# q of a linear-attention block for two tiles at a time, and the loop's order around it

## Chip, core and metric

The kernel runs on one core of one Trainium2 chip. The metric is the device time of one execution in microseconds. Five engines work at once and wait for each other by semaphores: TensorE (PE) multiplies, VectorE (DVE) and ScalarE (ACT) work on tiles in SBUF and read PSUM, GpSimd (POOL) does small steps and gathers, SyncE (SP) issues most of the DMAs. Each engine takes its instructions in program order.

## What is computed

A layer norm, a linear attention block with 32 heads on the normed rows, and a mixture-of-depths block on the raw rows: of 2048 tokens the eight with the highest score r go through a gated MLP. Both results and x are added.

```python
x = A_x                       # 1 x 2048 x 640, bf16
xn = layernorm(x)
# A: linear attention
q, k, v = split(xn @ wqkv)    # 32 heads of 20
phi = lambda t: where(t > 0, t + 1, exp(t)) + 1e-6
pq, pk = phi(q), phi(k)
kv = einsum("bhsd,bhse->bhde", pk, v);  z = sum over s of pk
o = (pq @ kv) / (pq . z + 1e-6);        a = o @ wo
# B: eight tokens
r = x @ w_r;  idx = the 8 tokens with the highest r
y = (silu(x[idx] @ w_gate) * (x[idx] @ w_up)) @ w_down * sigmoid(r[idx])
b = x + scatter_add(y at idx)
out = x + a + b
```

The kernel never forms v. It sums G = xn^T pk over all tokens and multiplies G with wv afterwards, so pk and xn of each tile feed PE's `ga`, `gb1` and `gb2` products.

## The kernel before

The 2048 tokens are 16 tiles of 128 rows (t = 0 to 15); the 640 columns are five chunks of 128. There is no scheduler: the order in which the program text issues instructions is the order on each engine. Tags of the PSUM pool name the banks: "A", "B" and "C" are pairs of banks (1024 fp32 columns), "D0" and "D1" single banks; each tag has one buffer, so a new tile in a tag waits until the old one has been read.

Stages, in order:

- **Loads** (L103 to L113): x tiles 0 to 7, wk, wq. Warm-up matmuls on zeros.
- **Layer norm of tile t**: `ln_half` (L160) is `bn_stats` on half a row, twice; `ln_aggr` (L165) aggregates to mean and variance (`mv`), then 1/sqrt: POOL adds eps (`sq`, L171), takes two powers (L176, L178) and copies the mean (`sc`, L179). For t < LN_FAST = 2 DVE adds eps, ACT copies the mean (L175), POOL takes one power and DVE the reciprocal (L189). `ln_stats` is both halves and the aggregate; `ln_norm` (L186) writes xn. For t >= 3 it also issues the DMA on SP that transposes xn into xnT (L196); tiles 0 to 2 are transposed on PE (`tr_tile`) and copied out (`tr_evict`).
- **The loop over tiles** (L341 on), with a start written out by hand for tiles 0 and 1. `k_mm` gives k and the score r in one go (641 columns, xnT is the stationary operand); `q_mm` gives q transposed, 25 matmuls of 128 columns with wq as stationary operand; `ga_mm(t)` adds xn^T pk for three of the five chunks. phi is exp and relu on ACT (`phi_act`), then min(exp, 1) + relu on DVE (`phi_vec`), into pk (rows) and pqT (columns of tokens).
- In a turn of the loop: PE takes k(t), ga(t-1), q(t). DVE takes the statistics of tile t+3 (t+4 behind turn CATCH = 5), the norm of t+2 (t+3), pqT(t-1), pk(t). ACT takes exp and relu of k(t), the score, exp and relu of q(t). SP takes the transpose of the newly normed tile and then one weight load of the plan in `late_loads` (L341). In turns 12 to 14 DVE adds xn to x (`residual`), and `keep` writes four such tiles to `xcp` in DRAM.
- **After the loop**: scores transposed (`pr`), top eight per block and over all (`rT`, `candm`, `pc`, `allc`, `idxi`), column sums of pk (`zp`, `zpart`, `zrel`), gb1, eight gathered columns on POOL (`xsT`), denominators (`pden`, `rden`, spread over DRAM by `rscr` and `rb`), gate and up (`gu`), gb2, down (`py`), an indirect DMA that adds y into xcp, reloads of x_sb, M = G wv wo per chunk.
- **Output**: `norm(j)` multiplies a block of pqT by rb; 16 tiles of pqT^T M, added to x_sb on DVE, stored.

The turn of the loop, which the change rewrites:

```python
    for t in range(2, T):
        kp = k_mm(t); ga_mm(t - 1); qp = q_mm(t)
        ln_stats(t + 3)      # t + 4 behind CATCH, both at it
        ln_norm(t + 2)       # t + 3 behind CATCH, both at it
        q_phi(t - 1, qer)
        ker = k_phi(t, kp)
        phi_vec(pk[:, t, :], ker, False)
        qer = phi_act(qp, "q")
        small_consts(t); late_loads(t)
```

Of the kernel before, what the change touches and what calls it, by code (L numbers as in the profile page):

```python
# [44 lines left out]
def kernel(  # L45
# [164 lines left out]
    def phi_act(ps, tag, between=None):  # L210
        e = work.tile([P, D], BF16, tag="e" + tag, name="e" + tag)
        r = work.tile([P, D], BF16, tag="r" + tag, name="r" + tag)
        nc.scalar.activation(e[:], ps[:, 0:D], AF.Exp)  # L213
# [2 lines left out]
        nc.scalar.activation(r[:], ps[:, 0:D], AF.Relu)  # L216
        return e, r

    def phi_vec(dst, er, as3):
        e, r = er  # L220
# [4 lines left out]
        nc.vector.scalar_tensor_tensor(  # L225
            out=dst, in0=ea, scalar=1.0, in1=ra, op0=ALU.min, op1=ALU.add
        )
# [175 lines left out]
    for t in range(2, T):
        kp = k_mm(t)
        ga_mm(t - 1)
        qp = q_mm(t)
        for u in (t + 3, t + 4) if t == CATCH else (t + 3 + (t > CATCH),):
            if u < T:
                ln_stats(u)
        for u in (t + 2, t + 3) if t == CATCH else (t + 2 + (t > CATCH),):  # L410
            if u < T:
                ln_norm(u)
        q_phi(t - 1, qer)
# [68 lines left out]
    nc.scalar.copy(GT[:, 0:2, 0:TBLK], two(gaC[:]))  # L482
# [270 lines left out]
    for t in range(T):  # L753
        o_t = work.tile([P, D], BF16, tag=("ek", "rk", "eq", "rq")[t % 4], name=f"o_t{t}")
        if t < T - 1:
# [6 lines left out]
            (nc.sync, nc.scalar)[t % 2].dma_start(out_v[:, t, :], o_t[:])  # L762
            if t == 4:
                norm(3)
        else:
            for i in range(3):
# [5 lines left out]
                (nc.scalar, nc.scalar, nc.sync)[i].dma_start(out_v[:, t, a:b], o_t[:, a:b])  # L772
# [34 lines left out]
```

## Time and profile before

| | us |
|---|---|
| median of 3 runs (lowest to highest) | 111.83 (111.79 to 111.94) |
| the profiled execution | 112.03 |
| its span (first to last instruction) | 110.3 |
| ScalarE busy in the span | 55.3 (50%) |
| GpSimd busy in the span | 38.9 (35%) |
| moved by DMA | 23.09 MB, 209 GB/s over the span |

The granted TensorE clock is full in all 40 slices of the page. In a line of the timeline the first number is the start in us from the start of the span, the second the time from there to the end of the (merged) instructions, then engine, line, operation, output and inputs, shapes and count; in brackets the idle time of the engine before it and who ended it. A line of the chain has the start, the time until the next link, engine, tile and line. A line of the groups has busy us and mean ns of one, then the idle time ahead of it. Lines of DMA issues have the size of one and the median us from issue to landing.

### The profile page before, as it was taken

How to read it: one execution, taken by the hardware profiler on the slowest of the kernel's cores; microseconds unless marked ns; L12 is line 12 of the kernel's file. 1: busy time of each engine (PE TensorE's matmuls, PEld its weight loads, DVE VectorE, ACT ScalarE, POOL GpSimd, SP SyncE). 2: the span in 40 equal slices, each digit the busy share in tenths (PEclk: the TensorE clock that was granted, in tenths of full speed). 3: DMA queues.
4: the chain of work that ended last, by engine and by line, in shares of the span. 5: the costliest groups of instructions: out<-in, count | busy, mean ns of one | idle time of the engine just before them, and what ended most of it. 6: DMA issues, size and time to landing. Idle time of an engine off the chain costs nothing.

```text
span 110.3 us, 3004 instructions
## 1 busy us (share of the span) xinstructions
PE 105.2 (95%) x1183; PEld 69.1 (63%) x1183; DVE 85.3 (77%) x197; ACT 55.3 (50%) x104; POOL 38.9 (35%) x89
## 2 busy tenths in 40 slices
PE   6988999999899999999999999999999999999990
PEld 2335867777577766777667744447996555555560
DVE  6687799988999889875999896951365986986680
ACT  4037987779577887777877755068026100000000
POOL 5426486789879955780000000250006000000000
PEclk9999999999999999999999999999999999999999
DMA  2998059989999998999999750019350499994333
GB/s 76 339 376 279 6 97 359 229 236 105 195 232 303 240 253 230 286 280 174 315 370 375 271 178 3 0 39 324 97 170 7 57 259 352 348 382 175 119 119 119
DMA packets 25358, 23.09 MB, mean 209 GB/s; under 512 B 10624, under 2 KB 24064, under 8 KB 25344
## 3 DMA queue, kind: packets, MB, share of 16 engines
q1 hardware_dynamic: 22784, 20.51, 67.4%
q10 hardware_dynamic: 2384, 2.35, 6.3%
q0 software_dynamic: 176, 0.04, 0.6%
q8 instruction: 9, 0.15, 0.5%
q14 instruction: 5, 0.04, 0.1%
HBM read 14.94 MB, written 5.81 MB: 188 GB/s over the span
## 4 chain that ended last, share of the span: by engine, by line
PE 70%; DVE 12%; DMA 7%; POOL 6%; issue 2%; DVEq 0%; POOLq 0%
PE o L743 14%; PE k L236 13%; PE q L248 13%; PE gbA L489 6%; DMA xnT<-xn 5%; PE gaC L259 4%; PE gbC L590 4%; DVE st L163 4%; POOL sq L176 3%; DVE xn L191 2%; PE gaD L259 2%; DMA x_sb<-in_A_x_dram 2%; PE M L728 2%; PE gu L606 2%; POOL sc L178 2%
## 5 line engine op out<-in xcount | busy, mean ns | idle before, releaser
L248 PEld LDWEIGHTS <-wq 128*128 128x128 bf16 x400 | 24.2, 117 | 3.4
L236 PE MATMUL k<-wk,xnT 128*128 128x512 bf16 (+1 forms) x160 | 24.8, 300 | 0.6 <-DMA xnT<-xn 0.3
L248 PE MATMUL q<-xnT,wq 128*128 128x128 bf16 x400 | 24.9, 219 | 0.0
L743 PEld LDWEIGHTS <-pqT 128*128 128x128 bf16 x165 | 12.7, 98 | 9.1
L236 PEld LDWEIGHTS <-xnT 128*128 128x128 bf16 x160 | 12.3, 98 | 8.9 <-ACT xnT L206 0.8
L213 ACT ACTIVATE eq<-q 128x640 bf16<-128x640 f32 x16 | 11.3, 704 | 10.1 <-PE q L248 10.1
L225 DVE SCALAR_TENSOR_TENSOR pk<-ek,rk 128x640 bf16<-128x640 bf16 x16 | 13.2, 823 | 3.1 <-ACT rk L216 2.9
L743 PE MATMUL o<-M,pqT 128*128 128x512 bf16 x110 | 15.6, 299 | 0.0
L163 DVE BATCH_NORM_STATS2 st<-x_sb 128x6 f32<-128x320 bf16 x32 | 14.2, 480 | 0.4 <-DMA x_sb<-in_A_x_dram 0.4
L176 POOL TENSOR_TENSOR sq<-sq,half 128x1 bf16<-128x1 bf16 x16 | 12.6, 787 | 4.2 <-DVE sq L171 3.0
L225 DVE SCALAR_TENSOR_TENSOR pqT<-eq,rq 128x640 bf16<-128x640 bf16 x16 | 13.2, 823 | 0.7 <-ACT rq L216 0.7
L213 ACT ACTIVATE ek<-k 128x640 bf16<-128x640 f32 x16 | 11.3, 705 | 2.0 <-PE k L236 1.0
L216 ACT ACTIVATE rq<-q 128x640 bf16<-128x640 f32 x16 | 11.2, 699 | 0.0
L216 ACT ACTIVATE rk<-k 128x640 bf16<-128x640 f32 x16 | 11.2, 698 | 0.0
L751 DVE TENSOR_TENSOR o_t<-o,x_sb 128x640 bf16<-128x640 f32 x11 | 8.9, 821 | 2.2 <-PE o L743 1.6
L537 POOL COPY xsT<-xnT 128x5 bf16 x8 | 2.3, 354 | 21.7 <-DVE icol L551 21.7
L178 POOL TENSOR_TENSOR sc<-sq,neg 128x1 f32<-128x1 bf16 x14 | 9.2, 657 | 1.1
L259 PE MATMUL gaC<-pk,xn 128*128 128x512 bf16 x32 | 9.5, 378 | 0.0
L191 DVE TENSOR_SCALAR xn<-x_sb,sc 128x640 bf16<-128x640 bf16 (+2 forms) x17 | 6.9, 412 | 2.4 <-POOL sc L179 2.1
L489 PE MATMUL gbA<-pk,xn 128*128 128x512 bf16 x32 | 7.3, 380 | 0.0
L171 POOL TENSOR_SCALAR sq<-mv 128x1 bf16<-128x1 bf16 x14 | 4.4, 313 | 7.4 <-DVE mv L167 7.4
L360 DVE TENSOR_TENSOR x_sb<-x_sb,xn 128x640 bf16<-128x640 bf16 x16 | 7.0, 482 | 0.0
(152 smaller groups left out, 118.7 us busy)
## 6 DMA issues: line engine op xcount, KB each, us to landing
xcp<-x_sb SPq DMA_DIRECT2D x4, 640.0 KB, 4.2
x_sb<-in_A_x_dram SPq DMA_DIRECT2D x3, 640.0 KB, 6.5
wd<-in_B_w_down_dram SPq DMA_DIRECT2D x2, 960.0 KB, 7.5
x_sb<-xcp SPq DMA_DIRECT2D x3, 640.0 KB, 6.5
wg<-in_B_w_gate_dram SPq DMA_DIRECT2D x2, 768.0 KB, 5.4
wu<-in_B_w_up_dram SPq DMA_DIRECT2D x2, 768.0 KB, 5.6
out_dram<-o_t SPq DMA_DIRECT2D x8, 160.0 KB, 3.3
out_dram<-o_t ACTq DMA_DIRECT2D x7, 160.0 KB, 3.4
```

Source lines behind the costliest of these rows:

```text
L163: nc.vector.bn_stats(out=stat[t][:, h, :], in_=x_sb[:, t, h * HW : (h + 1) * HW])
L176: nc.gpsimd.tensor_tensor(out=sq[:, 1:2], in0=sq[:, 0:1], in1=half[:], op=ALU.pow)
L178: nc.gpsimd.tensor_tensor(out=sc[:, 1:2], in0=sq[:, 1:2], in1=neg1[:], op=ALU.pow)
L191: nc.vector.tensor_scalar(out=xn[:, t, a:b], in0=x_sb[:, t, a:b], scalar1=sc[:, 0:1], scalar2=sc[:, 1:2], op0=ALU.subtract, op1=ALU.mult,)
L213: nc.scalar.activation(e[:], ps[:, 0:D], AF.Exp)
L216: nc.scalar.activation(r[:], ps[:, 0:D], AF.Relu)
L225: nc.vector.scalar_tensor_tensor(out=dst, in0=ea, scalar=1.0, in1=ra, op0=ALU.min, op1=ALU.add)
L236: nc.tensor.matmul(ps[:, a:b], lhsT=xnT[:, kc, t * P : (t + 1) * P], rhs=wk[:, kc, a:b], start=(kc == 0), stop=(kc == KC - 1),)
L248: nc.tensor.matmul(ps[:, m * P : (m + 1) * P], lhsT=wq[:, kc, m::KC], rhs=xnT[:, kc, t * P : (t + 1) * P], start=(kc == 0 and m in (0, 4)) ...
L259: nc.tensor.matmul(gaC[:, c * TBLK : (c + 1) * TBLK] if c < 2 else gaD[:], lhsT=xn[:, t, c * P : (c + 1) * P], rhs=pk[:, t, 0:TBLK], start ...
L489: nc.tensor.matmul(gbA[:, (c - 3) * TBLK : (c - 2) * TBLK], lhsT=xn[:, t, c * P : (c + 1) * P], rhs=pk[:, t, 0:TBLK], start=(t == 0), stop ...
L743: nc.tensor.matmul(ps, lhsT=pqT[:, m, t * P : (t + 1) * P], rhs=M[:, m, a:b], start=(m == 0), stop=(m == KC - 1),)
```

## The change

- `q_mm` for tiles 0 to 13 becomes `q2_mm`: one call makes q of tiles t and t+1, 25 matmuls with 256 moving columns, wq loaded once for both. The result (1280 columns) goes to pair B (`lo`, output chunks 0 to 3, 1024 columns) and bank D1 (`hi`, chunk 4, 256 columns). exp and relu on ACT and the sum on DVE are done per `lo` and `hi`.
- The loop takes two tiles in a turn (t = 2, 4, ..., 12); tiles 14 and 15 keep the old form. PE: k(t), lo(t), k(t+1), hi(t), ga(t-1), ga(t). DVE: pk(t-1), norms of t+2 and t+3, pqT of the pair before, statistics of t+4, pk(t), statistics of t+5. Turns 2 and 12 differ. `lo(t)` reads xnT of tiles t and t+1.
- LN_FAST goes from 2 to 4, and the fast form copies the mean on DVE, not on ACT.
- At the start, the second half of tile 1's statistics goes ahead of the norm of tile 0, tile 2 is normed ahead of pk(0), k(1) uses pair C and q of tiles 0 and 1 is one call.
- Residuals move: 0 to 4 in turn 12, 5 and 6 in turn 14, 7 to 10 in turn 15, 11 to 15 behind the top eight; the keeps are tiles 0 to 3, 4 to 7, 8 to 10, 11 to 15, the last two behind the loop.
- Loads: the x tiles 8 to 11 and 12 to 15 in slots 2 and 5 (1 and 3 before), wv in 12 and 13 (0 and 2), wo in 14 and 15 (4 and 5), wd in slots 16 and 17, issued behind `zrel` after the loop (12 and 13).
- The output stores swap queues: even tiles on ACT, odd ones on SP, the last three pieces on SP, ACT, SP.

```diff
-LN_FAST = 2
+LN_FAST = 4
-CATCH = 5
...
         if t < LN_FAST:
-            nc.scalar.copy(sc[:, 0:1], mv[:, 0:1])
+            nc.vector.tensor_copy(sc[:, 0:1], mv[:, 0:1])
...
+    def q2_mm(t, ps, ms):
+        for n, m in enumerate(ms):
+            for kc in range(KC):
+                nc.tensor.matmul(
+                    ps[:, n * 2 * P : (n + 1) * 2 * P],
+                    lhsT=wq[:, kc, m::KC],
+                    rhs=xnT[:, kc, t * P : (t + 2) * P],
+                    start=(kc == 0 and n % 2 == 0), stop=(kc == KC - 1),
+                    skip_group_check=True,
+                )
+        return ps
...
+    def q2_act(dst, func, ps, ms):
+        n = len(ms) * 2 * P
+        nc.scalar.activation(
+            dst[:, ms[0] : ms[-1] + 1, :].rearrange("p m f -> p (m f)"), ps[:, 0:n], func
+        )
+
+    def q2_vec(t, er, ms):
+        a, b = ms[0], ms[-1] + 1
+        nc.vector.scalar_tensor_tensor(
+            out=pqT[:, a:b, t * P : (t + 2) * P], in0=er[0][:, a:b, :], scalar=1.0,
+            in1=er[1][:, a:b, :], op0=ALU.min, op1=ALU.add,
+        )
+
+    LO, HI = (0, 1, 2, 3), (4,)
...
     ln_stats(0)
     ln_half(1, 0)
+    ln_half(1, 1)
     ln_norm(0)
+    ln_aggr(1)
     warm_mm(P, 3)
...
-    ln_half(1, 1)
-    ln_aggr(1)
...
         plan = {
-            0: (wv, wv_v, 0, 2), 1: (x_sb, x_v, 8, 12), 2: (wv, wv_v, 2, KC),
-            3: (x_sb, x_v, 12, 16), 4: (wo, wo_v, 0, 4), 5: (wo, wo_v, 4, 8),
+            2: (x_sb, x_v, 8, 12), 5: (x_sb, x_v, 12, 16),
             6: (wg, kcF, 0, 2), 7: (wg, kcF, 2, 4), 8: (wg, kcF, 4, 5),
             9: (wu, kcU, 0, 2), 10: (wu, kcU, 2, 4), 11: (wu, kcU, 4, 5),
-            12: (wd, kcD, 0, 6), 13: (wd, kcD, 6, 12),
+            12: (wv, wv_v, 0, 2), 13: (wv, wv_v, 2, KC), 14: (wo, wo_v, 0, 4), 15: (wo, wo_v, 4, 8),
+            16: (wd, kcD, 0, 6), 17: (wd, kcD, 6, 12),
         }
...
-    ln_stats(3)
+    ln_half(3, 0)
+    ln_norm(2)
+    ln_half(3, 1)
+    ln_aggr(3)
     ker = k_phi(0, kp)
-    kp = k_mm(1, "B")
-    qp = q_mm(0, "A")
-    ln_norm(2)
-    phi_vec(pk[:, 0, :], ker, False)
-    tr2 = bank("D1", "tr2").bitcast(BF16)
+    kp = k_mm(1, "C")
+    tr2 = bank("D0", "tr2").bitcast(BF16)
     tr_tile(2, tr2, 0, KC)
...
+    k_vec(0, ker)
     ln_norm(3)
     ln_stats(4)
+    ker = k_phi(1, kp, lambda: tr_evict(2, tr2, 0, KC, nc.scalar.copy))
+    lo = q2_mm(0, pair("B", "qlo0"), LO)
+    hi = q2_mm(0, bank("D1", "qhi0"), HI)
     ga_mm(0)
...
-    for t in range(2, T):
+    for t in range(2, T - 2, 2):
         kp = k_mm(t)
+        k_vec(t - 1, ker)
+        if t == 2:
+            ln_stats(5)
+            ln_norm(4)
+        else:
+            for u in (t + 2, t + 3):
+                ln_norm(u)
+        lo = q2_mm(t, pair("B", f"qlo{t}"), LO)
+        ker = k_phi(t, kp)
+        q2_vec(t - 2, eqp, LO)
+        q2_vec(t - 2, eqp, HI)
+        eqp = q2_tile("eq"), q2_tile("rq")
+        q2_act(eqp[0], AF.Exp, lo, LO)
+        if 2 < t < T - 4:
+            ln_stats(t + 4)
+        elif t == T - 4:
+            for u in range(3):
+                residual(u)
+        k_vec(t, ker)
+        kp = k_mm(t + 1)
+        hi = q2_mm(t, bank("D1", f"qhi{t}"), HI)
+        ga_mm(t - 1)
+        ga_mm(t)
+        ker = k_phi(t + 1, kp)
+        q2_act(eqp[1], AF.Relu, lo, LO)
+        q2_act(eqp[0], AF.Exp, hi, HI)
+        q2_act(eqp[1], AF.Relu, hi, HI)
+        if t == 2:
+            ln_norm(5)
+            ln_stats(6)
+        if t < T - 4:
+            ln_stats(t + 5)
+        else:
+            for u in range(3, 5):
+                residual(u)
+        for u in (t, t + 1):
+            small_consts(u)
+            late_loads(u)
+
+    for t in (T - 2, T - 1):
+        kp = k_mm(t)
+        if t == T - 2:
+            k_vec(t - 1, ker)
         ga_mm(t - 1)
         qp = q_mm(t)
...
+        residual(5 if t == T - 2 else 7)
+        k_vec(t, ker)
         qer = phi_act(qp, "q")
+        for u in (6,) if t == T - 2 else (8, 9, 10):
+            residual(u)
         late_loads(t)
+        keep(4 * (t + 2 - T), 4 * (t + 3 - T))
...
+    late_loads(T)
+    late_loads(T + 1)
...
-    for t in range(T - 4, T):
+    keep(T - 8, T - 5)
+    for t in range(T - 5, T):
         residual(t)
-    keep(T - 4, T)
+    keep(T - 5, T)
...
-            (nc.sync, nc.scalar)[t % 2].dma_start(out_v[:, t, :], o_t[:])
+            (nc.scalar, nc.sync)[t % 2].dma_start(out_v[:, t, :], o_t[:, 0:D])
...
-                (nc.scalar, nc.scalar, nc.sync)[i].dma_start(out_v[:, t, a:b], o_t[:, a:b])
+                (nc.sync, nc.scalar, nc.sync)[i].dma_start(out_v[:, t, a:b], o_t[:, a:b])
```

More of the change, by code (lines that the diff above doesn't have):

```diff
@@ L255, in q_mm, with q2_tile @@
         return ps
+    def q2_mm(t, ps, ms):
[9 more added lines that the diff above has]
+        return ps
+    def q2_tile(tag):
+        return work.tile([P, KC, 2 * P], BF16, tag=tag, name=tag)
+    def q2_act(dst, func, ps, ms):
[10 more added lines that the diff above has]
+    LO, HI = (0, 1, 2, 3), (4,)
     def ga_mm(t):
@@ L369, in q_phi, with k_phi, k_vec @@
         phi_vec(pqT[:, :, t * P : (t + 1) * P], er, True)
-    def k_phi(t, kp):
-        ker = phi_act(kp, "k")
+    def k_phi(t, kp, between=None):
+        ker = phi_act(kp, "k", between)
         nc.scalar.copy(r_all[:, t : t + 1], kp[:, D : D + 1])
         return ker
+    def k_vec(t, er):
+        phi_vec(pk[:, t, :], er, False)
     kp = k_mm(0, "A")
-    tr1a, tr1b = bank("D1", "tr1a").bitcast(BF16), pair("C", "tr1b").bitcast(BF16)
+    tr1a, tr1b = bank("D1", "tr1a").bitcast(BF16), pair("B", "tr1b").bitcast(BF16)
     tr_tile(1, tr1a, 0, 2)
@@ L405 @@
+    for t in (T - 2, T - 1):
+        kp = k_mm(t)
+        if t == T - 2:
+            k_vec(t - 1, ker)
         ga_mm(t - 1)
         qp = q_mm(t)
[L407 to L413, printed above, removed]
+        if t == T - 2:
+            q2_vec(t - 2, eqp, LO)
+            q2_vec(t - 2, eqp, HI)
+        else:
+            q_phi(t - 1, qer)
@@ L753 @@
     for t in range(T):
-        o_t = work.tile([P, D], BF16, tag=("ek", "rk", "eq", "rq")[t % 4], name=f"o_t{t}")
+        tag = ("ek", "rk", "eq", "rq")[t % 4]
+        o_t = work.tile([P, 2 * D if tag[1] == "q" else D], BF16, tag=tag, name=f"o_t{t}")
         if t < T - 1:
```

33 lines of the change are left out of this document (10 added, 23 removed).

## The prediction

> **What bounds the kernel now.** I read the page's busy shares first, then the chain of waits, then the timeline of the q/k loop.
>
> ```profile
> span 110.3 us, 3004 instructions
> ...
> PE 105.2 (95%) x1183; PEld 69.1 (63%) x1183; DVE 85.3 (77%) x197; ACT 55.3 (50%) x104; POOL 38.9 (35%) x89
> ```
>
> The span is TensorE (PE) work with 5 us of holes. The chain in order of time shows where it is that and where it is not:
>
> ```profile
> 18.57 0.81 DVE st L163 x2
> ...
> 19.61 0.31 DVE xn L191
> 19.92 0.73 DVE pqT L225
> ...
> 22.77 5.57 DMA xnT<-xn
> ...
> 28.39 1.56 PE k L236 x10
> ...
> 31.99 1.39 PE k L236 x10
> 33.37 0.43 PE gaC L259 x2
> ...
> 34.02 1.40 PE q L248 x25
> ...
> 55.98 1.38 PE k L236 x10
> ```
>
> From k(7) to the end of the loop PE never waits: a tile is 1.38 (k) + 0.65 (ga: the two on gaC 0.43, the third, on gaD, half of that) + 1.40 (q) = 3.43 us, and k(7) to k(14) give (55.98 - 31.99)/7 = 3.43. It is streaming, not weight loads: 25 q matmuls of 128 columns in 1.40 are 0.056 each, two of 512 in 0.43 are 0.216 each. The line through both gives 0.109 for 256 columns. Before k(6), at 28.39, there is one hole of about 0.45 us, where a transpose landed 5.57 us after its issue (k(4) at 21.07, quoted below, and two tiles would be 27.93). VectorE (DVE) at 77% follows PE, and what must be asked is whether it still does so after the change.
>
> **The change, part by part.**
>
> *256 columns.* Per pair 50 matmuls x 0.056 = 2.80 become 25 x 0.109 = 2.74. Bounds: no gain at all (2.80), or the 512-column rate, 25 x 0.108 = 2.70. I take 2.74: a pair of tiles costs PE 2 x 1.38 + 2.74 + 2 x 0.65 = 6.80 instead of 6.86. Seven pairs give at most 0.4 us. The 200 loads of wq that fall away lie under the stream and give nothing; if they did not, the streams above could not be so regular. ScalarE does per pair 2 x (1024 + 256) columns instead of 4 x 640:
>
> ```profile
> L482 ACT CAST GT<-gaC 128x1024 bf16<-128x1024 f32 x1 | 1.0, 1012 | 0.6 <-ACT zpart L475 0.6
> L213 ACT ACTIVATE eq<-q 128x640 bf16<-128x640 f32 x16 | 11.3, 704 | 10.1 <-PE q L248 10.1
> ```
>
> The line through the two rows gives 0.40 for 256 columns, 2 x (1.01 + 0.40) = 2.82 against 4 x 0.70 = 2.82: nothing. With k's 2 x (2 x 0.70) and a small copy it sits under PE's 6.80.
>
> The Trainium skill (TensorE: Matmul & The Clock Gate, Back-to-back issue gap) gives 81 ns as the sustained spacing of load and matmul at 128 columns. This trace has 56 ns, so the trace decides; by the page's figure 50 q matmuls would take 4.05 us where the chain shows 2.80.
>
> *Statistics and norms in twos.* This is where I see the price. In the steady pair loop DVE's order becomes: xn(t+2), xn(t+3), pqT of the last pair (1024, then 256 columns), st/mv(t+4), pk(t), st/mv(t+5), pk(t+1), and then xn(t+4), xn(t+5) again. xn(t+5) needs GpSimd (POOL) to have done the four small steps for t+4 and then for t+5; all of DVE is queued behind it: pqT, the next statistics, and pk, for which PE's ga waits. That closes a ring: mv(t+4), two POOL chains, xn(t+5), pqT, st, mv(t+6). Before, a chain had a whole tile of lead. POOL's steps are held up by DVE:
>
> ```profile
> 13.79 0.21 DVE L167 BATCH_NORM_AGGREGATE mv<-st 128x2 bf16<-128x12 f32 x1
> 13.91 0.77 DVE L225 SCALAR_TENSOR_TENSOR pk<-ek,rk 128x640 bf16<-128x640 bf16 x1
> 14.09 0.68 POOL L171 TENSOR_SCALAR sq<-mv 128x1 bf16<-128x1 bf16 x1 [1.61 <-DVE mv L167]
> 14.60 0.82 DVE L225 SCALAR_TENSOR_TENSOR pqT<-eq,rq 128x640 bf16<-128x640 bf16 x1
> 14.85 1.00 POOL L176 TENSOR_TENSOR sq<-sq,half 128x1 bf16<-128x1 bf16 x1
> ...
> 25.94 0.23 POOL L171 TENSOR_SCALAR sq<-mv 128x1 bf16<-128x1 bf16 x1
> 26.25 0.57 POOL L176 TENSOR_TENSOR sq<-sq,half 128x1 bf16<-128x1 bf16 x1
> ...
> 27.52 0.18 POOL L179 CAST sc<-mv 128x1 f32<-128x1 bf16 x1
> ```
>
> A POOL step that starts inside a pk or pqT ends about 0.15 (small step) or 0.5 (power) after DVE has passed on (0.68 and 1.00 where 0.23 and 0.57 are the free values). The free chain runs from 25.94 to 27.70, 1.76. The ring, counted from the start of mv(t+4) = 0:
> - pk(t) follows at 0.13 and lasts 0.73; the first small step falls into it and ends at 1.0. Two powers and the copy: 0.08 + 0.57 + 0.07 + 0.55 + 0.15, to 2.4.
> - DVE meanwhile: pk(t) to 0.87, st to 1.7, mv, pk(t+1) 1.86 to 2.6. The copy falls into that and ends at 2.7; xn(t+4) to 3.1.
> - Chain t+5 from 2.75, grazed by xn(t+4): to 4.4. xn(t+5) 4.45 to 4.8 (0.31 and its start).
> - pqT: no row has 1024 columns; 0.73 x 1024/640 = 1.17, less a fixed start, 1.13. Then 0.34 for 256 columns: 6.27. st 0.81: next mv at **7.1**.
>
> Against PE's 6.80 that is 0.3 a pair. Bounds: two free chains (3.5) and 0.3 to start, 0.4 for xn, 1.47, 0.85: 6.55, PE stays the bound; two chains of 2.0 each plus the first hold-up of 0.6, 7.6. I take 7.1. Five pairs (k(4) to k(14)) owe 1.55, less the lead that DVE starts with: walked in the same way from the start below, pk(4) is ready at 27.4 and PE comes to ga(4) at 27.75 (21.6 + 2 x 1.38 + 2.74 + 0.65), so 0.35: +1.2. PE saves 5 x 0.06 = 0.3 and the 0.45 hole (wv and wo leave the early queue, so the transposes have less ahead of them): **+0.45** in the loop.
>
> The Trainium skill (GPSIMD Engine Reference, Specifications) says that GpSimd's SBUF interfaces are shared with VectorE, with contention from instructions of two SBUF inputs. The trace agrees (0.68 and 1.00 under two-input pk and pqT). By that rule the ring is the 7.1; without it it would be the 6.55.
>
> *The start.* The order of the first tiles changes; tiles 2 and 3 take DVE's reciprocal.
>
> ```profile
> 6.59 1.56 PE L236 MATMUL k<-wk,xnT 128*128 128x512 bf16 x10
> 8.35 0.29 PE L200 MATMUL tr1a<-ident,xn 128*128 128x128 bf16 x2 [0.21 <-DVE xn L191]
> 9.10 1.56 PE L236 MATMUL k<-wk,xnT 128*128 128x512 bf16 x10 [0.30 <-ACT xnT L206]
> 12.51 0.45 DVE L191 TENSOR_SCALAR xn<-x_sb,sc 128x640 bf16<-128x640 bf16 x1 [0.59 <-POOL sc L179]
> ...
> 21.07 1.55 PE L236 MATMUL k<-wk,xnT 128*128 128x512 bf16 x10
> ...
> DMA to landing us min/median/max: 3.0/3.5/5.6
> ```
>
> The last line is the time to landing of the 13 transposes of xn. The mean's copy and half of st(1) now stand ahead of xn(0): k(0) some 0.13 later (an estimate), its stream of 1.37 over at 8.09. That half of st(1), 0.41, no longer stands ahead of xn(1), so the transposes of tile 1 follow at 8.09, not at 8.35, and k(1) 0.75 behind them (9.10 - 8.35): 8.84. Then k(1) 1.38, tr2 0.28 (5 x 0.056), q of tiles 0 and 1 2.74, ga 0.65, k(2) 1.38: lo(2) stands ready at 15.3. But it streams tile 3 too, which before was first needed by k(3), 3.4 us after k(2). xn(3), about 0.36 earlier, lets its transpose be issued at 12.6; 3.5 (the median) later is 16.1. PE waits 0.8. Bounds: 3.0 makes it 0.3, and 5.6 makes it 2.9; the queue is empty then, so I stay near the middle. k(4) at 21.6 against 21.07: **+0.5**. A shorter wait here would mostly be paid in the ring, which does not start earlier.
>
> *The end of the loop.* Residuals 8 to 10 now stand between pk(15) and the row of scores rT:
>
> ```profile
> 52.62 1.29 DVE L360 TENSOR_TENSOR x_sb<-x_sb,xn 128x640 bf16<-128x640 bf16 x3
> 62.15 0.83 DVE L225 SCALAR_TENSOR_TENSOR pk<-ek,rk 128x640 bf16<-128x640 bf16 x1 [0.15 <-ACT rk L216]
> 63.18 0.68 DVE L432 CAST rT<-pr 4x512 f32<-4x512 bf16 x1 [0.20 <-PE pr L430]
> 66.09 0.21 DVE L439 TENSOR_TENSOR candm<-split,selm 4x64 bf16<-4x64 bf16 x1
> 66.88 0.20 PE L499 MATMUL pc<-candm,ones 4*128 4x64 bf16 x1
> ```
>
> rT goes from 63.18 to 62.15 + 0.73 + 3 x 0.40 = 64.08, 0.9 later; candm had 0.58 of slack before pc, which PE takes in order: **+0.35** (0 if PE is late anyway, 0.9 if the slack is not there). What follows pc on DVE moves with it, and the gather of 8 tokens still precedes gu.
>
> *Late loads.* wd moves behind zrel (about 69 us), with the last keeps behind it on the same queue, then rscr and rb:
>
> ```profile
> wd<-in_B_w_down_dram SPq DMA_DIRECT2D x2, 960.0 KB, 7.5
> ...
> 81.62 1.01 PE L688 MATMUL py<-wd,hT 128*32 128x160 bf16 x48
> ...
> 84.79 1.56 DVE L737 CAST M<-M 128x640 bf16<-128x640 f32 x2 [1.34 <-PE M3a L728]
> ```
>
> wd lands near 77, py wants it at 81.6. What is queued ahead of rscr takes perhaps 2 us longer (an estimate from 7.5 us for 1.9 MB), and rscr had some of that to spare; norm(0), which waits for rb, may come 0.5 to 1.5 late. DVE's idle 1.34 us ahead of the M copies covers that: 0. If the cover fails it is 0.7. The other moved loads (wv, wo) are wanted only near 80 and later: 0.
>
> *Output queues.* The last three stores go to SP, ACT, SP:
>
> ```profile
> 107.20 0.85 ACTq L772 DMA_DIRECT2D out_dram<-o_t  x2
> 107.67 0.33 SPq L772 DMA_DIRECT2D out_dram<-o_t  x1
> ```
>
> The second no longer queues behind the first (0.43): **-0.15**, since the third then ends last.
>
> Sum: +0.5 + 0.45 + 0.35 - 0.15 = +1.15. The profiled execution took 112.03 (span 110.3 and 1.7 around it), so 113.2; the median of the runs is 0.2 lower: **113.0 us**.
>
> **The rivals.**
> - *PE stays the bound* (faster). GpSimd slips in between, ring 6.55, and tile 3's transpose lands in 3.0: start 0.0, loop -0.3 - 0.45, end +0.35, stores -0.15: -0.55, and -0.9 if candm keeps its slack. 111.3 down to 110.9. For it: the free chains at 26 us. Against: pk(t) stands directly behind mv(t+4), as at 13.91. With only half of this it is no change, 111.8.
> - *x_sb 8 to 11 is late* (slower still). It is now issued behind the transpose of tile 5, near 20.2, and st(8) wants it near 25.
>
> ```profile
> x_sb<-in_A_x_dram SPq DMA_DIRECT2D x1, 640.0 KB, 4.5
> ...
> x_sb<-in_A_x_dram SPq DMA_DIRECT2D x1, 640.0 KB, 6.5
> ```
>
> With 4.5 (issue at 15.22) it is in time, with 6.5 (at 21.20) DVE stops for 1.5 in the ring, which has no lead: +1.1 more, 114.1. A late norm(0) would add 0.7 in the same way.
> - *Weight loads pace q* (faster).
>
> ```profile
> L248 PEld LDWEIGHTS <-wq 128*128 128x128 bf16 x400 | 24.2, 117 | 3.4
> ```
>
> 175 of the 400 loads fall away; were they the bound, 24.2 x 175/400 = 10.6 us would go, 101.2. The regular 0.056 between the matmuls speaks against it. The 81 ns that the Trainium skill gives would come from such a bound.
>
> **How the numbers follow.** Forecast 0.50, late x_sb or norm(0) 0.20, PE bound with a gain 0.19, with none 0.10, weight loads 0.01. A change under 0.2%, 0.22 us, this measurement cannot tell. Faster 0.20, same 0.10, slower 0.70. The range reaches from the PE-bound case to the late load: 111.0 to 114.5; the forecast's own is 112.4 to 113.8.
>
> **What would show it.** In the loop: xn of a pair's second tile idle for POOL's copy by about a microsecond, ga of even tiles waiting for DVE pk, 7.1 us from k(6) to k(8) and on. At the start: lo(2) waiting for the transpose. At the end: pc waiting for candm. A loop of 6.8 us a pair, or DVE never idle for POOL, would refute the main step.

## The result, and the profile after

| | before | after |
|---|---|---|
| median of 6 runs each, us (lowest to highest) | 111.82 (111.77 to 111.94) | 115.32 (115.13 to 116.83) |
| span of the profiled execution, us | 110.3 | 113.6 |

The ratio is 1.0323, 95% interval 1.0271 to 1.0376. The kernel became slower, as forecast, but by 3.5 us where 1.2 were forecast, and the time lies outside the range. Two of the six runs after, at 116.8, had a granted clock of 0.985; the other four lie between 115.13 and 115.33. From the page after: the span, the busy shares, and the chain of waits by engine.

```profile
span 113.6 us, 2630 instructions
...
PE 105.9 (93%) x1008; PEld 68.3 (60%) x1008; DVE 85.8 (76%) x205; ACT 54.4 (48%) x102; POOL 35.8 (31%) x83
...
PE 29%; DVE 29%; POOL 21%; DMA 11%; issue 4%; ACT 2%; DVEq 0%; POOLq 0%; SPq 0%
```

TensorE is as busy as it was, but it is 29% of the chain that ended last. The rest is VectorE, GpSimd and DMA. Where the time is lost is found by putting the same steps of both timelines side by side; a row has the start, the time to the end of the merged instructions, engine, line and shapes. Before:

```profile
55.81 1.55 PE L236 MATMUL k<-wk,xnT 128*128 128x512 bf16 x10
...
75.00 0.59 SPq L621 DMA_DIRECT2D rscr<-rden  x1
78.38 0.88 SPq L625 DMA_DIRECT2D rb<-rscr  x2
81.97 1.48 DVE L632 TENSOR_TENSOR pqT<-pqT,rb 128x2560 bf16<-128x2560 bf16 x1
85.37 2.88 PE L743 MATMUL o<-M,pqT 128*128 128x512 bf16 x20
...
106.49 0.28 DVE L751 TENSOR_TENSOR o_t<-o14b,x_sb 128x128 bf16<-128x128 f32 x1
```

After:

```profile
20.74 1.55 PE L235 MATMUL k<-wk,xnT 128*128 128x512 bf16 x10
...
57.07 1.55 PE L235 MATMUL k<-wk,xnT 128*128 128x512 bf16 x10
68.56 0.20 PE L571 MATMUL pc<-candm,ones 4*128 4x64 bf16 x1 [0.33 <-DVE candm L509]
...
69.32 1.18 SPq L372 DMA_DIRECT2D wd<-in_B_w_down_dram  x2
70.60 5.17 SPq L392 DMA_DIRECT2D xcp<-x_sb  x2
76.68 0.59 SPq L694 DMA_DIRECT2D rscr<-rden  x1
83.27 0.87 SPq L698 DMA_DIRECT2D rb<-rscr  x2
86.89 1.49 DVE L705 TENSOR_TENSOR pqT<-pqT,rb 128x2560 bf16<-128x2560 bf16 x1 [3.17 <-DMA rb<-rscr]
88.44 3.25 PE L816 MATMUL o<-M,pqT 128*128 128x512 bf16 x20 [1.41 <-DVE pqT L705]
...
109.94 0.28 DVE L824 TENSOR_TENSOR o_t<-o14b,x_sb 128x128 bf16<-128x128 f32 x1
```

| reached | before | after | later by | of it new |
|---|---|---|---|---|
| k(4) | 21.07 | 20.74 | -0.33 | -0.33 |
| k(14) | 55.81 | 57.07 | 1.26 | 1.59 |
| pc | 66.88 | 68.56 | 1.68 | 0.42 |
| first o | 85.37 | 88.44 | 3.07 | 1.39 |
| piece o14b on DVE | 106.49 | 109.94 | 3.45 | 0.38 |
| end of span | 110.3 | 113.6 | 3.3 | -0.15 |

There are two large losses: 1.6 us in the loop of pairs, and 1.4 + 0.4 between pc and the first output tiles. The chain shows the first; its columns are start, length, engine, tile and line:

```profile
41.02 0.22 DVE mv L166
...
41.32 0.69 POOL sq L170
...
43.69 0.20 POOL sq L170
...
45.40 0.45 DVE xn L190
45.84 1.47 DVE pqT L279 x2
47.31 0.81 DVE st L162 x2
48.14 0.22 DVE mv L166
```

This is the ring of the prediction: from mv to the next mv 48.14 - 41.02 = 7.12 us, two GpSimd chains one behind the other and then xn, pqT and the statistics; the two turns ahead of it take 7.13 and 7.29. The second loss starts with rscr. Its issue is 1.68 us later than before, like everything behind pc, but rb, which needs it landed, is issued 6.6 us behind it where it was 3.4. The stretches of two us around it (the last two columns are the DMA share and GB/s):

```profile
68.00:70.00 2.00, 1.67 (x10) 0.71 (x9) 1.52 (x10) 1.47 (x3) 0.00 (x0) 1.00 0.10 4
...
72.00:74.00 2.00, 2.00 (x13) 0.75 (x12) 1.86 (x10) 0.00 (x0) 1.31 (x7) 1.00 1.04 379
...
78.00:80.00 2.00, 2.00 (x39) 2.00 (x37) 1.12 (x2) 0.55 (x2) 0.00 (x0) 1.00 1.07 394
```

From 66 to 70 us the DMA engines are nearly idle (a share of 0.07 to 0.10), from 70 to 72 half busy (0.57), then full to 82 (0.91 to 1.07). From 69.3 on wd (1.92 MB), the keeps (0.48 and 0.80 MB) and rscr (0.51 MB) stand in line on one queue: 3.7 MB.

### The profile page after: what moved, and what is told of

The parts are those of the page before. It is cut to its first block, busy times and chain, and to the rows that moved or that the text cites. A ratio compares the mean times of both kernels' runs of the same rounds, so it can differ in the third digit from the quotient of the medians.

```text
span 113.6 us, 2630 instructions
## 1 busy us (share of the span) xinstructions
PE 105.9 (93%) x1008; PEld 68.3 (60%) x1008; DVE 85.8 (76%) x205; ACT 54.4 (48%) x102; POOL 35.8 (31%) x83
## 4 chain that ended last, share of the span: by engine, by line
PE 29%; DVE 29%; POOL 21%; DMA 11%; issue 4%; ACT 2%; DVEq 0%; POOLq 0%; SPq 0%
PE o L816 14%; POOL sq L175 8%; DVE st L162 7%; DVE pqT L279 7%; POOL sc L177 6%; DMA rscr<-rden 6%; PE gbA L561 5%; POOL sq L170 4%; DVE xn L190 4%; DMA rb<-rscr 3%; POOL sc L178 3%; PE k L235 2%; DVE x_sb L389 2%; DMA x_sb<-in_A_x_dram 2%; DVE mv L166 2%
## 5 line engine op out<-in xcount | busy, mean ns | idle before, releaser
L259 PEld LDWEIGHTS <-wq 128*128 128x128 bf16 x175 | 18.5, 117 | 1.8 <-PE k L235 0.4
L235 PEld LDWEIGHTS <-xnT 128*128 128x128 bf16 x160 | 12.9, 98 | 10.2 <-ACT xnT L205 0.8
L259 PE MATMUL qlo<-xnT,wq 128*128 128x256 bf16 x140 | 16.4, 273 | 0.1
L175 POOL TENSOR_TENSOR sq<-sq,half 128x1 bf16<-128x1 bf16 x16 | 10.0, 626 | 6.6 <-DVE sc L174 4.5
L279 DVE SCALAR_TENSOR_TENSOR pqT<-eq,rq 128x1024 bf16<-128x1024 bf16 (+1 forms) x14 | 11.0, 824 | 0.0
L273 ACT ACTIVATE eq<-qlo 128x1024 bf16<-128x1024 f32 x7 | 7.2, 1023 | 5.8 <-PE qlo L259 5.8
L705 DVE TENSOR_TENSOR pqT<-pqT,rb 128x2560 bf16<-128x2560 bf16 x4 | 5.9, 1486 | 3.2 <-DMA rb<-rscr 3.2
L288 PEld LDWEIGHTS <-xn 128*128 128x128 bf16 x48 | 4.5, 97 | 6.1 <-issue 3.0
L177 POOL TENSOR_TENSOR sc<-sq,neg 128x1 f32<-128x1 bf16 x12 | 7.6, 630 | 0.9
L273 ACT ACTIVATE rq<-qlo 128x1024 bf16<-128x1024 f32 x7 | 7.4, 1052 | 0.0
```

What stands on the lines that cost most here:

```text
L175: nc.gpsimd.tensor_tensor(out=sq[:, 1:2], in0=sq[:, 0:1], in1=half[:], op=ALU.pow)
L177: nc.gpsimd.tensor_tensor(out=sc[:, 1:2], in0=sq[:, 1:2], in1=neg1[:], op=ALU.pow)
L235: nc.tensor.matmul(ps[:, a:b], lhsT=xnT[:, kc, t * P : (t + 1) * P], rhs=wk[:, kc, a:b], start=(kc == 0), stop=(kc == KC - 1),)
L259: nc.tensor.matmul(ps[:, n * 2 * P : (n + 1) * 2 * P], lhsT=wq[:, kc, m::KC], rhs=xnT[:, kc, t * P : (t + 2) * P], start=(kc == 0 and n % ...
L273: nc.scalar.activation(dst[:, ms[0] : ms[-1] + 1, :].rearrange("p m f -> p (m f)"), ps[:, 0:n], func)
L279: nc.vector.scalar_tensor_tensor(out=pqT[:, a:b, t * P : (t + 2) * P], in0=er[0][:, a:b, :], scalar=1.0, in1=er[1][:, a:b, :], op0=ALU.min ...
```

## The experiments

Each ratio is to the kernel before, run on the same chip, with its 95% interval. Theory: the loss is the ring in the loop, the residuals ahead of candm, and the queue ahead of rscr. Rivals stand with each.

### e1: wd in the last turn of the loop

```diff
+        if t == T - 1:
+            late_loads(T)
+            late_loads(T + 1)
...
-    late_loads(T)
-    late_loads(T + 1)
```

> The changed kernel with one thing undone: both halves of wd are issued in the last turn of the loop, as a step of SP ahead of the keep of tiles 4 to 7, and no longer behind zrel. Theory (late loads): in the changed kernel rscr (512 KB) takes 6.5 us to land where it took 3.2 before, because wd (1.9 MB) and two keeps stand ahead of it on SP's queue; norm(0) then waits 3.17 us for rb, and about 1.75 us of the loss come from there. With wd gone from ahead of them rscr lands in 3 to 4 us, norm(0) no longer waits for more than 0.5 us, and the time falls by 1.2 to 1.8 us, to 113.5 to 114.1; k(14) stays at 57.1 us. Rival (the norms are late only because everything ahead of them is, by 1.7 us, or because the keeps alone fill the queue): rscr still takes over 5.5 us and the time stays within 0.4 us of 115.3.

Measured 115.56 us, 1.0323 (1.0280 to 1.0366): nothing gained. Its timeline:

```profile
73.62 0.19 DVE L612 TENSOR_REDUCE zc<-zrel 128x5 f32<-128x20 f32 x1 [1.46 <-DMA zrel<-zpart]
74.94 2.05 DVE L389 TENSOR_TENSOR x_sb<-x_sb,xn 128x640 bf16<-128x640 bf16 x5
77.48 2.16 SPq L695 DMA_DIRECT2D rscr<-rden  x1
```

The wait only changed its place. wd, issued from 57.87 on behind wv and wo, lands 10.7 us after its issue, and the DMA engines are still full when zrel is issued at 67.26; zc waits for zrel, the five residuals behind zc start 1.6 us later than in the changed kernel (73.33), and their keep of 800 KB is issued directly ahead of rscr, which takes 5.8 us, so norm(0) again waits, 2.95 us. This left both readings open, the queue and the keep.

### e2 and e3: the ring

e2 moves pqT ahead of the two norms. e3 shortens GpSimd's chain to one power.

```diff
+        q2_vec(t - 2, eqp, LO)
+        q2_vec(t - 2, eqp, HI)
+        if t > 2:
             for u in (t + 2, t + 3):
                 ln_norm(u)
-        q2_vec(t - 2, eqp, LO)
-        q2_vec(t - 2, eqp, HI)
```

```diff
-LN_FAST = 4
+LN_FAST = 16
```

> The changed kernel with one move on VectorE: in the pair loop pqT of the last pair stands ahead of the two norms instead of behind them. Theory (ring): mv(t+4), two chains of GpSimd, xn(t+5), pqT, st, mv(t+6) is a ring of 7.1 to 7.3 us; pqT (1.5 us) leaves the part of it that waits and covers the chain. The ring falls to about 5.6, TensorE's 6.80 becomes the bound: k(14) comes 1.0 to 1.6 us earlier (57.07 now), xn of the second tile of a pair waits less than 0.3 us for GpSimd, and the time falls by 0.8 to 1.6 us, to 113.7 to 114.5, less what the late rscr keeps back. Rival (ScalarE's or TensorE's own order paces the loop at 7.2 us a pair, and VectorE's waits are a symptom): k(14) within 0.3 us of 57.07 and the time within 0.3 us of 115.3. Rival 2: pqT under the chain slows GpSimd's steps as pk does, the ring moves to another place and half of the gain stays.

> The changed kernel with LN_FAST 16: all tiles take the short form of 1/sqrt, in which VectorE adds eps, copies the mean and takes the reciprocal, and GpSimd takes one power only. Theory (ring through GpSimd's chain): a chain falls from 1.8 to 2.0 us to about 0.8 to 1.0, VectorE pays three small steps (about 0.3 us) a tile; the ring falls from 7.2 to between 5.8 and 6.6, TensorE's 6.80 is the bound, k(14) comes 0.6 to 1.4 us earlier than 57.07 and the time falls by 0.4 to 1.3 us. Rival (GpSimd is not what xn waits for, VectorE's own work of a pair is the bound): the added steps make the pair 0.3 to 0.6 us longer, k(14) 1.5 us later or more, the time above 116.

Measured: e2 113.38 us, 1.0129 (1.0094 to 1.0164); e3 113.36 us, 1.0121 (1.0086 to 1.0157). Both gained more than their ranges said (up to 1.6 and 1.3 us). In e2's timeline, then e3's:

```profile
21.11 1.55 PE L235 MATMUL k<-wk,xnT 128*128 128x512 bf16 x10
...
35.47 1.55 DVE L279 SCALAR_TENSOR_TENSOR pqT<-eq,rq 128x1024 bf16<-128x1024 bf16 x2
35.57 1.20 POOL L170 TENSOR_SCALAR sq<-mv 128x1 bf16<-128x1 bf16 x1
38.25 0.53 DVE L190 TENSOR_SCALAR xn<-x_sb,sc 128x640 bf16<-128x640 bf16 x1 [0.87 <-POOL sc L178]
...
55.47 1.55 PE L235 MATMUL k<-wk,xnT 128*128 128x512 bf16 x10
```

```profile
20.79 1.55 PE L235 MATMUL k<-wk,xnT 128*128 128x512 bf16 x10
...
55.28 1.55 PE L235 MATMUL k<-wk,xnT 128*128 128x512 bf16 x10
```

From k(4) to k(14) the changed kernel takes 36.33 us, e2 34.36, e3 34.49 (20.79 to 55.28): 6.87 and 6.90 us a pair. Either end of the ring, loosened, brings TensorE back as the bound; the rival that ScalarE or TensorE paces the loop falls. The wait for GpSimd did not go below 0.3 in e2 as I expected (0.87 is left: a small step that starts under pqT lasts 1.20 us), but nothing waits behind it any more. e2's time fell by 1.9 us, more than the 1.6 at k(14): norm(0) also starts 3.0 us behind the issue of rb, not 3.6. In e3 that is 3.5.

### e4: residuals 8 to 10 behind the top eight

```diff
-        for u in (6,) if t == T - 2 else (8, 9, 10):
+        for u in (6,) if t == T - 2 else ():
...
+    for t in range(T - 8, T - 5):
+        residual(t)
     keep(T - 8, T - 5)
```

> The changed kernel with residuals 8 to 10 moved from the last turn of the loop to behind the top eight, right ahead of the keep that writes them. Theory: they delay rT and candm on VectorE, and pc waits 0.33 us for candm; without them pc comes about 0.4 us earlier (68.56 now), the column sums and rscr follow, and the time falls by 0.2 to 0.5 us. Rival (the rscr queue sets what comes behind): pc is earlier, but the later keep stands nearer to rscr on the queue and the time changes by less than 0.2 us, or grows by up to 0.5.

Measured 114.80 us, 1.0265 (1.0225 to 1.0306): 0.5 us less. Its timeline:

```profile
65.52 1.28 PE L532 MATMUL zp<-pk,ones_bf 128*32 128x512 bf16 x32
68.57 0.20 PE L571 MATMUL pc<-candm,ones 4*128 4x64 bf16 x1
```

From zp to pc 3.05 us, as before (63.83 to 66.88); in the changed kernel it is 3.45 (65.11 to 68.56). The residuals cost 0.4. pc itself is no earlier in this profile, since everything from k(0) on is 0.4 later in it (6.88 against 6.46), and its span is 0.6 us shorter since norm(0) starts 3.0 us behind the issue of rb (3.6 in the changed kernel), as in e2. So the time alone does not show the 0.4, the rows do; why rb lands sooner in some executions stays open.

### e5 and e6: the loads, from both sides

e5 moves the loads of the changed kernel forward, so that nothing is issued behind zrel; e6 puts wd behind zrel in the kernel before.

```diff
-            2: (x_sb, x_v, 8, 12), 5: (x_sb, x_v, 12, 16),
+            2: (x_sb, x_v, 8, 12), 4: (x_sb, x_v, 12, 16), 5: (wv, wv_v, 0, KC),
...
-            12: (wv, wv_v, 0, 2), 13: (wv, wv_v, 2, KC), 14: (wo, wo_v, 0, 4), 15: (wo, wo_v, 4, 8),
-            16: (wd, kcD, 0, 6), 17: (wd, kcD, 6, 12),
+            12: (wd, kcD, 0, 6), 13: (wd, kcD, 6, 12), 14: (wo, wo_v, 0, 4), 15: (wo, wo_v, 4, 8),
```

```diff
-            12: (wd, kcD, 0, 6), 13: (wd, kcD, 6, 12),
+            16: (wd, kcD, 0, 6), 17: (wd, kcD, 6, 12),
...
+    late_loads(T)
+    late_loads(T + 1)
```

> The changed kernel with the load plan moved forward and nothing else: x tiles 12 to 15 in slot 4, all of wv (800 KB) in slot 5, wd in slots 12 and 13, wo in 14 and 15, no load behind zrel. Theory (queue: rscr lands late because 1.9 MB of wd and 1.28 MB of keeps stand ahead of it on SP's queue, and zrel must not stand behind wd either, which is what the run with wd in the last turn of the loop did wrong): the queue is empty when zrel is issued near 67.2, zrel lands in under 2.6 us, rscr lands about 80.6 instead of 83.2, norm(0) starts near 84.3 instead of 86.9, within the cover of 1.3 us that VectorE has there, and the time falls by 1.4 to 1.9 us, to 113.4 to 113.9. Rival A (the 800 KB keep directly ahead of rscr does it alone, as in that run): rscr still takes over 5.5 us and less than 0.6 us is gained. Rival B (earlier loads slow the transposes in the loop): k(14) later than 57.4 and the gain is given back there.

> The kernel before with one part of the change alone: both halves of wd are issued behind zrel after the loop. Theory (queue): 1.9 MB of wd and 640 KB of the last keep stand ahead of rscr, which lands near 79.7 instead of 78.2, so norm(0) starts 1.2 to 1.8 us later than 81.97; VectorE's idle time ahead of the M copies covers 1.3 of it, and the time grows by 0.1 to 0.6 us, to 111.9 to 112.4. That would also say that wd alone is a small part of what the changed kernel loses there, and that the larger keep (11 to 15) and the later start of it do the rest. Rival (wd late is the whole loss): 1.3 us or more, above 113.1. Rival 2 (cheaper transposes in the loop pay for it): the time falls.

e5: 113.83 us, 1.0120 (1.0067 to 1.0174), 1.5 us less than the changed kernel, with k(14) unmoved at 57.18. e6: 112.31 us, 1.0003 (0.9958 to 1.0048), no change. Their timelines, e5 first:

```profile
85.24 1.49 DVE L702 TENSOR_TENSOR pqT<-pqT,rb 128x2560 bf16<-128x2560 bf16 x1 [1.41 <-DMA rb<-rscr]
87.06 2.98 PE L813 MATMUL o<-M,pqT 128*128 128x512 bf16 x19
```

```profile
82.89 1.49 DVE L634 TENSOR_TENSOR pqT<-pqT,rb 128x2560 bf16<-128x2560 bf16 x1 [0.99 <-DMA rb<-rscr]
85.15 2.89 PE L745 MATMUL o<-M,pqT 128*128 128x512 bf16 x19
```

Measured against pc, norm(0) starts 15.09 us behind it in the kernel before (81.97 - 66.88), 16.15 in e6 (pc at 66.74), 16.58 in e5 (pc at 68.66) and 18.33 in the changed kernel. So wd alone makes norm(0) 1.1 us late, the keeps behind the loop alone 1.5 (the last of them is larger and nearer to rscr than before), both together 3.2. The 1.34 us in which VectorE idled ahead of the M copies cover either, but not both: the first o starts 18.41 us behind pc in e6 and 18.40 in e5, as before (18.49), but 19.88 in the changed kernel. In e2 and e4, with the same transfers in line as in the changed kernel, it is 19.3: the delay at the first o is 0.8 to 1.4 us, depending on the execution.

### e7: the stores alone, in the kernel before

```diff
-            (nc.sync, nc.scalar)[t % 2].dma_start(out_v[:, t, :], o_t[:])
+            (nc.scalar, nc.sync)[t % 2].dma_start(out_v[:, t, :], o_t[:])
...
-                (nc.scalar, nc.scalar, nc.sync)[i].dma_start(out_v[:, t, a:b], o_t[:, a:b])
+                (nc.sync, nc.scalar, nc.sync)[i].dma_start(out_v[:, t, a:b], o_t[:, a:b])
```

> The kernel before with the change of the output queues alone (even tiles on ACT, odd ones on SP, the last three pieces on SP, ACT, SP). The prediction's term: the time falls by 0.1 to 0.2 us, 111.65. Rival: issues of stores on ACT hold up ACT's own work in the output stage and nothing is gained, or up to 0.3 us is lost.

Measured 111.92 us, 0.9973 (0.9936 to 1.0010): inconclusive by the time alone. The profile is finer: from the o14b piece on DVE to the end of the span it is 110.3 - 106.49 = 3.8 us before, 110.8 - 107.14 = 3.7 in e7 and 113.6 - 109.94 = 3.7 after. With the span read to 0.1, that agrees with 0.15 and cannot say more.

### e8 to e14: mended versions

e8 has e2's order, e5's loads, residuals 0 to 9 in twos between the two norms of a pair (where VectorE waited), the rest in turns 12 and 14, and the last two keeps behind zrel.

```diff
-            for u in (t + 2, t + 3):
-                ln_norm(u)
+            ln_norm(t + 2)
+            residual(t - 4)
+            residual(t - 3)
+            ln_norm(t + 3)
...
+    keep(T - 8, T - 4)
+    keep(T - 4, T)
```

> The changed kernel with the three causes taken away together: pqT of the last pair ahead of the norms; the load plan with wv in slot 5 and wd in 12 and 13; residuals in twos between the two norms of a pair, where VectorE waits for GpSimd, the rest in the turns 12 and 14, and the last two keeps (tiles 8 to 11 and 12 to 15) right behind zrel. Theory: k(14) at 55.2 to 55.8 (55.81 before), pc no longer waits for candm, rscr lands in under 4 us, o starts at 84.9 to 85.3 (85.37 before), stores as in the changed kernel: 110.9 to 111.6 us, a little faster than the kernel before. Rival (the residuals hold up GpSimd's steps as pk does, and the ring is back): xn of the second tile waits over 1 us, transposes of the second tile land late for lo, k(14) after 56.5 and the time above 112.

Measured 112.78 us, 1.0042 (1.0005 to 1.0079): outside its forecast, better than the changed kernel, no better than the one before. One wait stands out:

```profile
36.64 1.56 PE L235 MATMUL k<-wk,xnT 128*128 128x512 bf16 x10 [1.27 <-DMA xnT<-xn]
```

That is k(8). The transpose of tile 8 stands behind 1.44 MB of x and wv. e9 spreads the loads and has ACT issue all four zrel copies; e10 is its twin with 128 columns.

```diff
+            2: (x_sb, x_v, 8, 12), 3: (wv, wv_v, 0, 2),
+            4: (x_sb, x_v, 12, 16), 5: (wv, wv_v, 2, KC),
+            6: (wg, kcF, 0, 2), 7: (wg, kcF, 4, 5), 8: (wg, kcF, 2, 4), 9: (wu, kcU, 4, 5),
+            10: (wu, kcU, 0, 2), 12: (wu, kcU, 2, 4), 13: (wd, kcD, 0, 6),
+            14: (wd, kcD, 6, 12), 15: (wo, wo_v, 0, 8),
...
-            (nc.sync if i < 3 else nc.scalar).dma_start(
+            nc.scalar.dma_start(
```

```diff
-                nc.tensor.matmul(
-                    ps[:, n * 2 * P : (n + 1) * 2 * P],
...
-                    rhs=xnT[:, kc, t * P : (t + 2) * P],
+                for h in range(2):
+                    nc.tensor.matmul(
+                        ps[:, (2 * n + h) * P : (2 * n + h + 1) * P],
...
+                        rhs=xnT[:, kc, (t + h) * P : (t + h + 1) * P],
```

> The kernel with the three causes mended, with the loads spread more evenly (at most 1.2 MB a turn up to turn 10, where 1.44 MB in one turn made the transpose of tile 8 land late and k(8) wait 1.27 us; wu's second part, wd and wo in turns 12 to 15), and with all four zrel copies issued by ACT, not three of them by SP. Theory: the loads were all that kept that kernel from its loop of 6.80 us a pair and from an early zrel: no k waits over 0.3 us for a transpose, k(14) at 55.2 to 55.7, o starts at 84.6 to 85.2, time 0.5 to 1.3 us under the kernel before on the same chip (ratio 0.988 to 0.996). Rival (transposes collide with any load here, wherever it stands): a k or lo waits 0.5 us or more at another tile and the time is 0 to 1 us over the kernel before.

> The same kernel as the one with the loads spread, with q for two tiles as 50 matmuls of 128 columns in place of 25 of 256, order and all else the same: the 256 columns alone. The prediction's term: 2.80 against 2.74 us a pair, 0.06 x 7 = 0.4 us slower than its twin. Rival 1 (nothing: the smaller number of matmuls is hidden by a wait): within 0.1 us. Rival 2 (the loads of wq pace q): 50 loads and matmuls take over 3.5 us a pair where every weight is loaded twice in a row, and the time grows by 5 us or more.

Measured: e9 114.25 us, 1.0169 (1.0117 to 1.0222); e10 114.16 us, 1.0154 (1.0104 to 1.0204). e9 missed: it is slower than the kernel before, not faster. e10 is not slower than its twin, as its rival 1 had it. e10's loads:

```profile
zrel<-zpart ACTq DMA_DIRECT2D x4, 2.5 KB, 5.6
```

About 6 MB were issued from 54.5 us on, and the four zrel copies took 5.6 us to land from ACT's own queue, which was otherwise empty; VectorE waited 2.83 us for them. In e1 the single copy on that queue took 5.7, in the kernel before 2.0. Another queue did not get it past full DMA engines. e11 goes back to e8's plan and halves wv only (parts in slots 3 and 5); e12 is its twin with 128 columns.

> The kernel with the three causes mended (zrel on SP again, wd in slots 12 and 13, wo in 14 and 15), with wv in two parts in slots 3 and 5 and not in one in slot 5: the 1.44 MB of loads in one turn that made the transpose of tile 8 land 5 us late become 0.96 and 1.12 MB. Theory: k(8) no longer waits 1.27 us, every pair takes 6.80 us, k(14) at 55.4 to 55.8, zrel and rscr land as in that kernel (its tail needs no more), and the time falls by 1.0 to 1.4 us against it: ratio to the kernel before 0.990 to 0.997. Rival (the transposes collide with the loads at another tile): a k waits over 0.5 us elsewhere, ratio 1.000 to 1.006.

> The same kernel with q for two tiles as 50 matmuls of 128 columns instead of 25 of 256: the 256 columns alone, in a loop that TensorE bounds. Theory (streaming): 6.87 us a pair against 6.80, so 0.4 to 0.5 us slower than its twin, ratio to the kernel before 0.995 to 1.001. Rival (the loop is bound by the ring or by transposes after all): the same time as its twin within 0.1 us.

Measured: e11 112.28 us, 0.9988 (0.9959 to 1.0018); e12 112.26 us, 0.9983 (0.9949 to 1.0016). Neither is faster than the kernel before beyond the interval, and e12 takes the same time as its twin, as its rival had it. k(8) no longer waits, but in e11's timeline two other waits show:

```profile
42.22 1.56 PE L235 MATMUL k<-wk,xnT 128*128 128x512 bf16 x10 [0.28 <-DMA xnT<-xn]
...
55.56 0.38 PE L288 MATMUL gaC<-pk,xn 128*128 128x512 bf16 x1 [0.24 <-DVE pk L224]
```

k(10) stands behind 1.5 MB of wg, and the last ga behind pk(12), which stands behind three residuals. e13 takes both away; e14 is its twin with 128 columns.

```diff
+            2: (x_sb, x_v, 8, 12), 3: (wv, wv_v, 2, KC), 4: (x_sb, x_v, 12, 16), 5: (wv, wv_v, 0, 2),
+            6: (wg, kcF, 0, 2), 7: (wg, kcF, 2, 3), 8: (wg, kcF, 3, 5), 9: (wu, kcU, 0, 1),
+            10: (wu, kcU, 1, 3), 11: (wu, kcU, 3, 4), 12: (wu, kcU, 4, 5),
+            13: (wd, kcD, 0, 6), 14: (wd, kcD, 6, 12), 15: (wo, wo_v, 0, 8),
...
-        elif t == T - 4:
+        k_vec(t, ker)
+        if t == T - 4:
             for u in range(10, 13):
                 residual(u)
-        k_vec(t, ker)
...
+    keep(4, T - 8)
```

> The mended kernel with two more waits taken away: wg and wu in parts so that no turn loads more than 1.15 MB, and residuals 10 to 12 behind pk(12). The keep of tiles 4 to 7 goes behind zrel, so that zrel finds less ahead of it. Theory: every pair takes 6.80 us, k(14) at 55.0 to 55.4 (55.81 before), pc near 66.3, o near 84.8, and the time falls by 0.4 to 0.9 us against the kernel before on the same chip: ratio 0.992 to 0.997. Rival (transposes meet a load anyway, or rscr meets the third keep): a k waits 0.4 us or more, or rscr takes over 4 us, and the ratio stays at 0.998 to 1.003.

> Its twin with q for two tiles as 50 matmuls of 128 columns: 6.87 us a pair, k(14) 0.35 us later, the time 0.3 to 0.5 us longer. Rival (another bound hides it): within 0.1 us of its twin.

Measured: e13 111.74 us, 0.9959 (0.9922 to 0.9996); e14 111.95 us, 0.9976 (0.9941 to 1.0010). e13 is the only version whose interval lies below 1, by little: 0.4% in the ratio over all runs, 0.14 us between the medians (the runs before spread from 111.63 to 113.37), and it is the best of several. It has the stores of e7, which alone gave 0.9973, so no gain of q in twos is shown. e13's timeline, then e14's, then e12's:

```profile
22.64 2.35 PE L259 MATMUL qlo<-xnT,wq 128*128 128x256 bf16 x20
24.83 1.55 PE L235 MATMUL k<-wk,xnT 128*128 128x512 bf16 x10
...
35.33 1.55 PE L235 MATMUL k<-wk,xnT 128*128 128x512 bf16 x10
...
55.76 1.56 PE L235 MATMUL k<-wk,xnT 128*128 128x512 bf16 x10
...
106.39 0.28 DVE L822 TENSOR_TENSOR o_t<-o14b,x_sb 128x128 bf16<-128x128 f32 x1
```

```profile
22.13 2.40 PE L260 MATMUL qlo<-xnT,wq 128*128 128x128 bf16 x40
24.36 1.55 PE L235 MATMUL k<-wk,xnT 128*128 128x512 bf16 x9
```

```profile
49.79 1.55 PE L235 MATMUL k<-wk,xnT 128*128 128x512 bf16 x10
...
56.64 1.55 PE L235 MATMUL k<-wk,xnT 128*128 128x512 bf16 x10
```

e13's pairs from k(8) to k(14) take (55.76 - 35.33)/3 = 6.81 us. k(14) still stands at 55.76 and not at 55.4, since k(4) came at 21.26 there, 0.5 us later than in the changed kernel, and the first two pairs took 6.96 and 7.11. Piece o14b is 0.10 us earlier than before (106.39 against 106.49) and the end of the span 0.3 (110.0 against 110.3): in these two profiles most of the little that is gained lies in the stores.

lo takes 2.19 us with 256 columns (0.110 each) and 2.23 with 128 (0.056 each), 0.04 us a pair and 0.01 for hi. Pairs in which PE waits for nothing say the same: 6.79 to 6.81 us with 256 columns (e2, e11, e13), 6.85 to 6.87 with 128 (e10, e12; above, k(12) to k(14) of e12). The rows thus give about 0.4 us over seven pairs. The times of the twins differ by -0.1, 0.0 and +0.2 us (e10, e12, e14 against theirs), and their profiles have other waits in the loop (e14's pairs take up to 7.25 us, its ga waiting for pk), so the times can neither show nor exclude it.

## Why the prediction was wrong in size and right in direction

- **256 columns: right.** 0.110 us each where 0.109 was taken, and a pair is 0.06 us shorter where nothing else waits, as forecast. The loads of wq pace nothing: with twice as many (350 in e14, 175 in e13) the stream takes the same time, to 2%. By the change 175 of the 400 loads fall away, as the rival has it, and not the 200 of the part on 256 columns. The Trainium skill (TensorE: Matmul & The Clock Gate, Back-to-back issue gap) gives 81 ns as the sustained spacing at 128 columns; e14's 0.056 us contradicts it, so the trace decides.
- **The ring: right in mechanism, nearly in size.** The turn above takes 7.12 us, 7.1 forecast; e2 and e3 show it from two sides. Over k(4) to k(14) it owed 36.33 - 34.00 = 2.3 us against 6.80 a pair, where the sum had 1.2. Of the 1.1 more, 0.86 would be the start: k(4) came at 20.74, not 21.6, and the ring, by the prediction's own argument, does not start earlier; no run separates this share. The Trainium skill (GPSIMD Engine Reference, Specifications) has the interfaces shared with VectorE; the 1.20 us of a small step under pqT, and 0.69 under pk, agree.
- **The start: wrong in sign.** 3.5 us was taken for tile 3's transpose, the median of before. In the emptier queue it is less, from the rows that write xnT in the changed kernel:

```profile
DMA to landing us min/median/max: 2.6/2.7/4.9
```

  lo(2) starts at 15.32, not at 16.1, and k(4) was 0.33 us early instead of 0.5 late. Of the 0.33, 0.13 is k(0) (6.46 against 6.59), which comes at 6.46 to 6.88 us in the profiles with this start at a full clock; from k(0) to k(4) it is 14.28 us after and 14.48 before. Start and loop together: 1.26 measured, 0.95 forecast, and that the two sums are so close is luck: two misses cancel in part.
- **End of the loop: right.** 0.42 measured, 0.35 forecast; e4 gives 0.40.
- **Late loads: the step that failed.** It was costed at nothing: a queue about 2 us longer ahead of rscr, norm(0) 0.5 to 1.5 us late, and VectorE's idle 1.34 us as cover, or 0.7 if the cover fails. The mechanism was named, the size was not worked out. Counted from pc, norm(0) was 3.2 us late, and the cover left 1.4 at the first o and 0.4 in the first output tiles: 1.8 us. The prediction took its size from wd alone, for which "nothing" is nearly true (e6: the first o no later, 0.2 us in the output tiles); it named the last keeps in that line, but did not charge them: the last one is 160 KB larger and issued only 1.3 us ahead of rscr (at 75.4, behind the five residuals), and the keep of tiles 8 to 10 is new there. 3.7 MB at the 379 GB/s of the row above are 9.8 us, which from the first full stretch at 72 end near 82; rscr landed at 83.2 (issued at 76.68, 6.5 us). The sizes and the rate (382 GB/s at most) stood on the page before; only the start at 72 had to be estimated.
- **x tiles 8 to 11 late: did not come.** No statistics waited for them; the loss in the loop is gone in e2 with these loads unmoved.
- **Stores: -0.15**, as forecast, within what the rows can tell.

In the sum: 0.95 + 0.35 + 0 - 0.15 = 1.15 forecast, 1.26 + 0.42 + 1.77 - 0.15 = 3.3 measured. The late loads are 1.8 of the 2.1 us by which it missed; in an execution like e2's or e4's they would be 1.2.

## What to carry to other kernels

A moved DMA is costed by the whole line that it joins (the bytes issued since the DMA engines were last idle, over the rate that the profile shows, give when the small transfer behind them lands, here to about a microsecond), and an idle stretch that covers one delay does not cover two. Work grouped in twos to save the engine that is the bound can join two latencies into one ring on engines that are not, so the ring is written down and a step looked for (here pqT) that can be put under its waiting part. A larger matmul in place of two is worth only what the streams differ by, here 0.05 to 0.06 us in 6.8, less than any one wait that the reordering added.
